# A hand-laid instruction order rewritten, with the last output projections of the first tile in two parts

## The chip, the core and the metric

The kernel runs on one core of a Trainium2 chip. The metric is the device time of one execution in microseconds (us). The work is spread over TensorE (PE: matrix products, with PEld for the loading of weights), VectorE (DVE), ScalarE (ACT) and GpSimd (POOL); SyncE (SP) issues nearly all DMA transfers. Each engine takes its instructions in program order and waits at an instruction until what it needs is there.

## What is computed

An attention over keys and values that are averaged over groups of eight, and behind it two gated layers. The weights but one arrive as float64, all else as float32; the products are fp32 products, or sums of three products of high and low parts.

```python
k_p = k.reshape(B, H, Sp, 8, D).mean(axis=3); v_p = ...   # B, H, S, D = 4, 8, 576, 64
attn = softmax(q @ k_p.T / sqrt(D)); x = attn @ v_p        # x becomes 2304 x 512
xn = x / sqrt(mean(x * x) + 1e-6) * rms_g
g, val = xn @ w_gate, xn @ w_val                           # 512 -> 1536
x = (silu(g) * val) @ w_out                                # 1536 -> 512
out = ((x @ w_a) * (x @ w_b)) @ w_out2                     # 512 -> 1536 -> 512
```

## The kernel before

Tokens are taken in blocks of 128 (S0 to S17). The first layer works on them in four stretches: a first tile of 512 tokens, a second of 256, and two slices of 768 (`TILES1`). The second layer then takes three slices of 768.

The two stages up to the second layer are written out by hand. `FIRST` (line 129) and `SECOND` (line 31) are lists of tokens; `token` (line 778) runs one token after another, and the instructions that a token makes join the queues of their engines in that order. So a list sets, for each engine and for the DMA queue of SyncE, the order of its work, and nothing else reorders it (`manual_schedule`, from line 1598). Waits come from the data alone. The parts of a token's name:

- `K`, `L`, `y`, `z` load the keys and values of batch 0 to 3, `q` a block of queries, `l` one weight part (lines 265 to 380 and 596). `k`, `w` sum keys and values of batch 0 by eights on VectorE (`w0!` on GpSimd), `b` and `t` spread them into blocks; `p`, `r`, `u` are the same steps of the later batches. `N` makes the negated identity (line 749). `W` is the warming: products of the identity with itself into two banks (line 754).
- `S` followed by block and step is attention of a block: `.0` scores (PE), `.1` maximum (DVE; from block 4 on also the difference), `.8` subtraction of the maximum as a product (PE, blocks 0 to 3), `.2` exponential (ACT), `.3` transposes (PE), `.4` their copy (ACT), `.5` values (PE), `.6` division (DVE), `.7` squares (ACT), `R` the root (DVE), `.9` scaling (DVE), `.10` transposes (PE), `.11` high part (ACT), `.12` low part (DVE). A trailing `a` or `b` is half of such a step, `@acc0` and the like name the PSUM bank it borrows.
- `c0` to `c3` convert one weight part from float64 (line 609): two ScalarE instructions, two on VectorE (`c1`, `c2`, lines 637 and 649), and an addition (`c3`, line 656) on GpSimd, or on VectorE where the token ends in `!`. There are 36, three for each of the 12 pieces of the hidden layer: gate, value, output. `D` writes a converted output weight back to memory.
- `s`f`.0h`, `s`f`.0l` split a gate weight into a high part (ScalarE, line 692) and a low part (line 696: GpSimd, or VectorE with `!`); `s`f`.1` is the value weight.
- `g`, `v` are the gate and value products of a job of the first tile, in two halves `a` and `b` of three products for each of two pieces (line 706); `a` is the gate's activation, `h` its product with the value on VectorE, `o` the output projection: fp32 products of four pieces (line 711). There are 14 jobs: pieces 0 and 1 in halves of 256 tokens (jobs 0 to 3), pieces 2 to 11 whole (jobs 4 to 13).

In `SECOND`, `G`, `V`, `A`, `H`, `W`, `Y`, `O` are the same work for the second tile (line 1325; here the output projection takes parts, and a low part of an output weight is `W`f`l`), `E` copies out the first tile's result, `M` and `N` are the products of the two slices, `Q` and `U` their output projections (`Qe`, `Ue` copy a bank out, line 1564), `Z` prepares the second layer, and `||` opens the stage of the slices with banks of its own (line 1610). A bank of PSUM is placed in the order in which its name is first used in a stage.

An `!` moves a step to the other of GpSimd and VectorE (or a copy from ScalarE to VectorE, line 259).

## Time and profile before

| | us |
|---|---|
| median of three runs | 955.52 |
| the three runs | 953.97, 955.52, 955.97 |
| the profiled execution | 956.15 |
| its span, first to last instruction | 954.4 |
| TensorE busy in that span | 932.6 |
| mean granted clock of TensorE | 0.997 of 2.4 GHz |

The profiled execution's time lies 1.75 us above its span (the start and the end around it), and 0.63 us above the median. A row of a timeline gives the start from the span's beginning, the duration, the engine and the line of the kernel, what is written from what, and in brackets how long the engine was idle before it and what ended that. Neighbouring instructions of one form are merged (x8), and a fp32 product makes two records. Matrix products overlap, so a row's end is later than the next row's start.

### The profile page before, as it was taken

To read this page: it belongs to the slowest core of one execution; us is meant where nothing else is said; L and a number is where in the kernel's file an instruction comes from. 1 tells how busy PE (TensorE), PEld (TensorE's weight loads), DVE (VectorE), ACT (ScalarE), POOL (GpSimd) and SP (SyncE) were. 2 spreads that over 40 slices of the span, in tenths; PEclk is the share of its full clock that TensorE was granted. 3 is DMA by queue.
4 is the path that set the end of the run, shared out by engine and by line. 5 is a ranking of instruction groups with operands and counts; after the bars stand their busy time and mean duration, and the time that the engine had idled before them with its cause. 6 is when DMAs were issued, how large, how long until landed. Compare 5 with 4: busy or idle time off the path is not lost. (4 is left out here: it accounts for less than half of the span.)

```text
span 954.4 us, 14742 instructions
## 1 busy us (share of the span) xinstructions
PE 932.6 (98%) x5242; PEld 852.4 (89%) x5242; DVE 630.4 (66%) x1094; ACT 486.4 (51%) x943; POOL 342.2 (36%) x319
## 2 busy tenths in 40 slices
...
GB/s 293 198 248 265 176 81 130 172 127 42 48 58 72 42 174 122 143 76 154 149 223 106 154 104 150 131 140 127 142 154 136 127 116 229 183 165 100 157 108 66
DMA packets 67944, 133.34 MB, mean 140 GB/s; under 512 B 7456, under 2 KB 31264, under 8 KB 67872
## 3 DMA queue, kind: packets, MB, share of 16 engines
...
q8 instruction: 41, 0.67, 0.3%
q10 hardware_dynamic: 288, 0.39, 0.1%
...
## 5 line engine op out<-in xcount | busy, mean ns | idle before, releaser
L1203 DVE TENSOR_TENSOR hl<-hf,hh 128x768 fp32r<-128x768 f32 x36 | 35.5, 991 | 90.9 <-ACT hh L1202 90.9
L1225 PE MATMUL o<-wol,hh 128*128 128x512 f32 x216 | 84.0, 389 | 0.0
L1225 PE MATMUL o<-woh,hh 128*128 128x512 f32 x216 | 84.0, 389 | 0.0
L1225 PE MATMUL o<-woh,hl 128*128 128x512 f32 x216 | 84.0, 389 | 0.0
L1202 ACT CAST hh<-hf 128x768 fp32r<-128x768 f32 x36 | 30.0, 838 | 82.0 <-PE o L1225 74.6
L656 POOL TENSOR_TENSOR w<-w,st 128x512 int32<-128x512 int32 x20 | 26.2, 1309 | 113.1 <-DVE w L649 111.9
L1559 PE MATMUL o<-hh,wol 128*128 128x512 f32 (+1 forms) x192 | 65.1, 339 | 0.4 <-DVE wol L1533 0.4
L1559 PE MATMUL o<-hl,woh 128*128 128x512 f32 (+1 forms) x192 | 64.6, 337 | 0.5 <-DVE hl L1546 0.5
L1559 PE MATMUL o<-hh,woh 128*128 128x512 f32 (+1 forms) x192 | 64.8, 337 | 0.0
L1130 ACT COPY p<-X 128x384 f32<-128x384 f32 x36 | 17.3, 481 | 88.7 <-PE X L1122 88.7
L696 POOL TENSOR_TENSOR wl<-wf,wh 128x512 fp32r<-128x512 f32 x25 | 35.5, 1425 | 49.7 <-ACT wh L692 40.4
L656 POOL TENSOR_TENSOR wo<-wo,st 128x512 int32<-128x512 int32 x18 | 24.3, 1349 | 67.3 <-DVE wo L649 38.9
L626 ACT ACTIVATE st<-st 128x512 int32<-128x512 uint32 x72 | 48.2, 670 | 0.0
L1225 PEld LDWEIGHTS o<-woh,hh 128*128 128x128 f32 x216 | 40.6, 188 | 8.4
L1225 PEld LDWEIGHTS o<-wol,hh 128*128 128x128 f32 x216 | 40.6, 188 | 8.3
L1225 PEld LDWEIGHTS o<-woh,hl 128*128 128x128 f32 x216 | 40.6, 188 | 8.3
L714 PE MATMUL acc<-ht,wo 128*128 128x512 f32 (+1 forms) x112 | 43.0, 531 | 0.0
L1122 PE MATMUL X<-xh_t,bl 128*128 128x384 f32 x120 | 40.8, 340 | 1.2 <-DVE bl L1487 0.7
L1122 PE MATMUL Y<-xh_b,rl 128*128 128x384 f32 x120 | 41.1, 342 | 0.9 <-ACT p L1427 0.7
L1122 PE MATMUL X<-xh_b,al 128*128 128x384 f32 x120 | 40.5, 337 | 1.5 <-DVE ev L261 1.5
L1122 PE MATMUL X<-xh_t,rl 128*128 128x384 f32 x120 | 40.6, 338 | 1.0 <-ACT u L1130 1.0
L1158 DVE TENSOR_TENSOR u<-u,Y 128x384 f32<-128x384 f32 x36 | 19.8, 550 | 32.3 <-ACT u L1130 15.4
...
## 6 DMA issues: line engine op xcount, KB each, us to landing
...
```

What stands on the lines that cost most here:

```text
L626: nc.scalar.activation(out=low, in_=low.bitcast(U32), func=AF.Copy, scale=2.0 ** -29)
L656: (nc.vector if boot["alt"] else nc.gpsimd).tensor_tensor(out=bits, in0=bits, in1=low, op=ALU.add)
L696: (nc.vector if boot["alt"] else nc.gpsimd).tensor_sub(wl, wf[ph, f, i], wh.bitcast(F32))
L714: nc.tensor.matmul(accs[c][:, cols], w[:, c, :], ht[:, :cols.stop - cols.start], start=(f == 0 and cols.start == 0), stop=(f == NF - 1),)
L1122: nc.tensor.matmul(dst[:, :HALF], w[:, c0 + c, :], x[:, c, :], start=(start and i == 0), stop=(stop and i == 5), skip_group_check=True,)
L1130: nc.scalar.copy(t, src[:, :HALF])
L1158: nc.vector.tensor_add(u2, u2, Y[:, :HALF])
L1202: nc.scalar.copy(hh, hf)
L1203: nc.vector.tensor_sub(hl, hf, hh.bitcast(F32))
L1225: nc.tensor.matmul(accs[i], x[:, sub], y, start=(f == 0 and j == 0), stop=(f == NF - 1 and j == 2),)
L1559: nc.tensor.matmul(dst, w[:, c, :], x, start=(f == 0 and j == 0 and at == 0), stop=(f == NF - 1 and j == 2), skip_group_check=True,)
```

## The change

Both lists are laid out anew. `FIRST` has the same tokens and twelve more; `SECOND` has the same tokens. In both some tokens gain or lose their `!`: in `FIRST` 17 instead of 12 low parts of gate and value weights are on VectorE, in `SECOND` 8 instead of 4 low parts of output weights, and `t2`, the last of the mask products, goes to GpSimd. The last three output projections of the first tile (jobs 11 to 13) take high and low parts of weight and hidden value: `s9.2`, `s10.2`, `s11.2` split the weights, `x` and `y` the hidden values, into spare buffers of the tiles of x. `WARM` goes from 20 to 17; the loop makes `WARM // 2` products for each of two banks. The cut lists below show `FIRST` whole, and of `SECOND` the beginning, the change of stage and the end.

```diff
-WARM = 20
+WARM = 17
...
 SECOND = """
-y0 y1 r0 y2 B0 r1 S6.0 G0a s13.0h s13.1h W0c r2 S6.1 y3 G0b s13.1l! B1 E1 E0 S6.2 s13.0l S7.0 E0>
-V0a E2 s14.0h V0b S7.1 r3 y4 S6.3 E1> E2> S7.2 S6.4 y5 r4 S7.3 S7.4 S6.5 A0 E3 G1a S6.6 G1b y6 E3>
-S7.5 H0 s14.1h Y0c W0l B2 s15.0h Y0l S7.6 V1a r7 s14.0l W1c V1b s14.1l A1 H1 S8.0 B3 W1l! Y1c G2a
-s15.0l G2b q9 r8 S8.1 r5 V2a S6.7 A2 s16.0h O0a s15.1h S7.7 s15.1l! S9.0 Y1l! q10 S9.1 V2b G3a z0
...
-M0.e4 Ft1l! Fd1 || M0.3 M0.1 M1.1 Fd2 S13.3 M0.cr M0.p1 M1.e1 M1.3 M0.d1 M0.lr! S13.4 S12.3 M0.2
-T2> M1.e2! S12.4 Ft2c Fb11c Ft2l M1.e3 M1.cs M1.e4 M1.p1 S13.5 S13.6 q15 M0.4 Ft3c Fb11l M0.p5
...
-U11.x U11.h0 U11.k0 U10.4 U11.1 Zb11l U11.0 U11.k1! Ue0! Zt3l Zt2l U11.4 Zt4c Z0.la Ue0> Zt4l U11.2
-Ue1 Ue1> Ue2! U11.3 Ue3 Ue4 U11.5 Ue5 Ue5> Ue4> Ue2> Ue3> Z0.lb
+S6.0 s13.1h y0 E0! S6.1 s13.0h S7.0 r0 S6.2 G0a G0b B0 y1 B1 S7.1 E1! E0> E2 y2 r1 B2 s13.0l s13.1l
+S6.3 W0c S7.2 E2> S6.4 V0a S7.3 s14.0h E1> S7.4 s14.0l y3 A0 W0l E3 V0b r2 r3 H0 S6.5 G1a s14.1h
+W1c B3 s14.1l S6.6 G1b Y0c s15.0h V1a V1b q9 S7.5 Y0l! E3> y4 S7.6 A1 H1 G2a G2b y5 s15.0l! S8.0
+W1l q10 s15.1h S6.7 Y1c V2a s15.1l! B4 B5 S8.1 O0a r7 O0b r8 s16.0h S9.0 A2 Y1l! W2c S8.2 s16.0l!
+q11 S7.7 O1a O1b V2b S9.1 W2l H2 S8.3 r4 S9.2 G3a R6! G3b S8.4 S9.3 W3c r5 V3a V3b y6 s16.1h Y2c
...
+T0 T1 M0.e3 S13.3 M0.ls! Fd1 T3 S13.4 || M0.cr M1.e1 M0.1 M1.1 M1.e2 M0.2 M0.lr! q14 T1> Ft2c Fb11l
+M1.cs M1.ls! M0.3 M1.3 M1.e3 Ft2l M1.p1 M2.e1 T0> M1.e4 M0.p1 Ft3c M2.e2 M0.p5 S12.3 T3> T2> M1.2
...
+U10.k1! U9.5 U11.f2 U10.x! U10.h0 U9.2 U11.h1 U10.5 U11.h0 U10.k0 U11.w Z0.lr! U10.2 U11.k1! U10.1
+U10.3 Z1.ls! U10.0 U11.k0! U11.x! U11.1 U10.4 Zt2l! U11.0 Ue0 U11.2 U11.5 U11.3 U11.4 Ue1 Ue2 Ue0>
+Ue3! Ue4! Ue5! Zt4c Ue3> Z0.ls Ue5> Z1.lb Zt4l Ue4> Ue1> Ue2>
 """.split()
 FIRST = """
-K0 K1 W N k0 K2 K3 k1 k2 k3 b1a K4 b1b b0a q1 S0.0a@att S0.1a b0b S0.0b S1.0a@acc0 S1.1a S1.0b
-S1.1b S0.8a K5 w0! S0.1b w1 S1.8a q2 S0.2a S1.8b t0! S1.2a S0.8b S1.2b l K6 S2.0@acc1 L0 S0.2b t1!
-l w2 c0 S0.3a@acc0 c1 c2 t2 p0 l L1 S1.3a@att S1.3b S0.3b q3 S0.4a S0.4b c0 S0.5a@acc0 S1.4a S2.1
-S0.5b S2.8 c0 S1.4b l c3 c1 S2.2a S1.5a@att S2.2b c2 c1 S1.5b S2.3a@acc1 l S0.6 p1 G c2 S1.6 S0.7
-S2.3b S3.0@acc0 c3 S3.1 S2.4a c0 S1.7 c1 s0.1h R0 c2 S3.8 s0.0h l S0.9 S2.4b S3.2a S2.5a@att
-S3.3a@acc1 c0 S3.2b S0.10@v c3 c1 S0.11 c3 S1.9 q4 L2 S2.5b L3 S3.4a s0.0l s0.1l c2 S3.3b p2
-S1.10@g S3.5a@acc0 S3.4b S3.5b S1.11 l S0.12 p3 S1.12 c0 S2.6 g0a s1.0h p7 S2.7 g0b v0a p8 S3.6
-S3.7 s1.0l! v0b a0 R2 c3 q5 S4.0@acc1 c0 h0 S2.9 g1a g1b s1.1h S2.10@att S3.9 s1.1l! S3.10@acc0
-S2.11 a1 c1 S3.11 v1a v1b S2.12 c2 S5.0@att q6 S3.12 g2a h1 c1 c2 l L4 c0 D0 g2b a2 S4.1 l c1 c0 c1
-c2 c3 L5 v2a v2b h2 l c3 s2.0h c3! g3a c2 c3! l c0 o0 c1 l g3b a3 c2 D1 v3a s2.1h l s2.0l c3! v3b
-g4a D2 o1 c0 g4b s3.0h h3 s2.1l! v4a c0 c0 c1 q7 a4 c2 p4 v4b c1 l c3 c2 c1 c0 s3.0l g5a s3.1h l
-g5b c3! o2 c2 l c1 D3 c3! s3.1l! c2 c0 h4 s4.0h c3! c1 c0 o3 c2 c1 c2 v5a a5 l c3! s4.0l p5 v5b c0
-s4.1h l L6 S4.2 l c0 c3 l h5 c1 g6a c2 o4 S5.1 s4.1l! g6b v6a c3 c1 c2 l v6b c3! c0 c0 l c1 c2
-s5.0h s5.0l! a6 c3! g7a c0 q8 c1 g7b c2 s5.1h s6.0h c3! o5 D4 h6 s5.1l! c1 l c0 c1 s6.0l! l c2 v7a
-c3 s6.1h c2 c0 c0 c3! S4.3@att l c1 v7b c1 a7 s7.0h D5 c2 s6.1l! c3 c2 g8a S5.2 D6 c0 c3 h7 g8b
-s7.0l! a8 p6 l s7.1h c0 l c0 s7.1l c1 v8a c2 c3! v8b h8 l c1 g9a c2 c0 S4.4 p9 o6 l c1 g9b c3!
-S4.5@att s8.1h v9a c0 s8.0h l a9 c1 c2 c2 c0 c3 s8.0l! l c1 v9b S4.6 c2 g10a c1 s8.1l S5.3@att h9
-c3 s9.0h g10b S5.4 c0 D7 c3 S5.5@att c2 l D8 a10 v10a v10b c1 c2 s9.1h S4.7 S5.6 s9.0l l c3! o7
-S5.7 R4 c3! c0 l c1 S4.9 l c2 g11a c0 g11b c3! c0 s10.0h h10 s9.1l S5.9 c1 c1 S4.10@att s10.0l
-S4.11 c2 v11a v11b S4.12 c0 a11 s10.1h g12a c3! c2 s10.1l D10 c3 l o8 h11 c0 S5.10@att S5.11 c1 D9
-s11.0h g12b c2 c1 a12 v12a c3! v12b s11.1h c2 c3 s11.0l! s12.1h g13a o9 D11 g13b s11.1l s12.0h h12
-S5.12 o10 v13a a13 v13b o11 h13 o12 s12.1l o13 s12.0l
+K0 k0 K1 k1 W K2 q1 k2 K3 b0a b1a k3 b1b S0.0a@att S1.0a@acc0 K4 N l b0b S0.1a q2 S1.0b c0 S0.8a
+S1.1a S0.0b S1.1b S0.1b S1.8a K5 S0.2a l K6 S1.2a l S0.8b S1.8b c1 S0.2b w0! c2 S0.3a@acc1 S0.4a w1
+c3 c0 t0! L0 S2.0@att S1.2b S0.3b S2.1 S0.4b w2 c1 G c0 l p0 S1.3a@acc0 L1 S2.8 S0.5a@acc1 t1!
+S1.4a s0.0h c1 c2 t2! S1.3b S2.2a c2 S2.2b q3 c3 S0.5b S1.5a@att S1.4b l S2.3a@acc0 s0.1h S0.6
+S1.5b p1 S1.6 S2.3b S2.4a S3.0@acc1 S3.1 S2.4b L2 c3 S0.7 S1.7 p2 S3.8 R0 c0 L3 S2.5a@att q4 S3.2a
+S3.3a@acc0 s0.0l S2.5b c1 c0 S0.9 S0.10@v S1.9 c2 S3.2b S3.4a S0.11 l S3.3b c1 l S1.10@g S1.11
+S3.4b c3 c0 p3 S0.12 q5 s0.1l S3.5a@acc1 S3.5b S1.12 S2.6 s1.0h L4 p7 g0a p8 S2.7 S3.6 g0b q6 S3.7
+v0a c2 c3! s1.0l R2 a0 S4.0@acc0 v0b h0 g1a s1.1h S2.9 c0 g1b s1.1l! q7 l S2.10@att v1a S2.11 S3.9
+c1 S3.10@acc1 S3.11 S2.12 c2 a1 c0 S3.12 v1b S5.0@att g2a S4.1 c3 c1 L5 h1 g2b l o0 c2 a2 c0 v2a c1
+c3! l v2b c1 c2 g3a o1 c3! c0 c2 l h2 l s2.0h c3! D0 l c1 g3b s2.1h s2.0l! v3a c0 c2 s2.1l! c1 c3!
+a3 c2 c0 v3b q8 l s3.0h h3 g4a c3! l c1 g4b v4a v4b s3.1h c0 s3.0l! s3.1l a4 p4 c1 g5a c2 c0 S5.1
+c3 c1 c2 c2 g5b D1 c0 h4 S4.2 c3 S5.2 s4.0h o2 s4.0l! c1 v5a a5 c3 l l c0 l c2 v5b c0 c3! s4.1h l
+c1 c2 c1 c3 g6a c2 S4.3@att c3 c0 o3 s5.0h s4.1l! D2 l l S4.4 g6b c1 a6 h5 c2 c3! o4 c0 c0 v6a
+s5.1h s5.0l! c0 s5.1l v6b c1 l c0 g7a p5 c1 c2 h6 c1 g7b c2 D3 c2 c3 L6 p6 l v7a c3 l v7b o5 s6.0h
+a7 s6.1h c3! l c1 D4 s6.0l c2 p9 c0 c3! s7.0h c0 c1 g8a D6 S4.5@att g8b D5 s6.1l! c2 c3 c0 h7
+s7.0l! v8a a8 c1 c2 c3! l S4.6 v8b l c0 c1 c0 c2 l c3! S5.3@att g9a c1 s7.1h s7.1l c2 c3 h8 S5.4
+S5.5@att c1 c0 s8.0h o6 S5.6 s8.1h s8.0l! S5.7 l g9b c1 c2 l S4.7 c0 v9a c1 c3! l D8 c2 c3! c0 v9b
+c2 s8.1l! R4 c1 a9 s9.0h s9.0l! g10a S4.9 c2 g10b h9 c0 c3! s9.1h c1 S5.9 l l o7 v10a s9.1l!
+S4.10@att v10b c0 c2 c3 c1 a10 c0 g11a c2 l h10 c3! S4.11 c1 S4.12 c3! c2 s10.0h c3! g11b s9.2h l
+a11 s10.1h c0 v11a s10.2h s10.0l v11b c1 c0 c2 l h11 s10.1l! g12a c3 c1 c2 o8 x11 s11.0h D7 c0
+s10.2l S5.10@att g12b a12 v12a s12.0h c1 v12b y11 o9 s11.0l g13a h12 c3 S5.11 x12 s9.2l S5.12 D9
+o10 s11.1h s11.1l! c2 D10 g13b o11 s12.1h c3! s11.2h y12 v13a s12.0l! v13b a13 s12.1l! h13 x13 D11
+o12 y13 s11.2l o13
 """.split()
...
             ht = state[j, "ht"]
             nc.vector.tensor_mul(ht[:, :m], ht[:, :m], state[j, 1][:, :m])
 
+        def spare():
+            if "spare" not in state:
+                state["spare"] = [
+                    x_p.tile([P, KD, 512], F32R, tag=tag, name=f"parts_{tag}") for tag in ("xh", "xl")
+                ]
+            return state["spare"]
+
+        def out_part(j, low):
+            f = jobs[j][0]
+            base = 2 * (j % 2)
+            hi, lo = [
+                spare()[0][:, base + e].rearrange("p (c f) -> p c f", c=KD) for e in range(2)
+            ]
+            if not low:
+                nc.scalar.copy(hi, wf[0, f, 2])
+                state[j, "w"] = (hi, lo)
+            else:
+                (nc.vector if boot["alt"] else nc.gpsimd).tensor_sub(lo, wf[0, f, 2], hi.bitcast(F32))
+
+        def hidden_part(j, low):
+            hi, lo = [spare()[1][:, 2 * (j % 2) + e] for e in range(2)]
+            if not low:
+                nc.scalar.copy(hi, state[j, "ht"])
+                state[j, "x"] = (hi, lo)
+            else:
+                nc.vector.tensor_sub(lo, state[j, "ht"], hi.bitcast(F32))
+
         def project_out(j):
             if not accs:
                 accs.extend(new_accs())
             f, cols, last = jobs[j]
+            if (j, "x") in state:
+                (wh, wl), (hh, hl) = state[j, "w"], state[j, "x"]
+                for c in range(KD):
+                    for i, (w, x) in enumerate(((wl, hh), (wh, hh), (wh, hl))):
+                        nc.tensor.matmul(
+                            accs[c], w[:, c, :], x, start=False, stop=(f == NF - 1 and i == 2)
+                        )
+                return
             out_direct(wf[0, f, 2], f, accs, state[j, "ht"], cols)
 
         for j in range(len(jobs)):
             names[f"v{j}b"] = lambda j=j: half(j, 1, 2)
             names[f"h{j}"] = lambda j=j: hidden(j)
             names[f"o{j}"] = lambda j=j: project_out(j)
+            for e in range(2 if j > 7 else 0):
+                names[f"s{jobs[j][0]}.2{'hl'[e]}"] = lambda j=j, e=e: out_part(j, e)
+                names[f"{'xy'[e]}{j}"] = lambda j=j, e=e: hidden_part(j, e)
         for i in range(2):
             for f in range(2 * NF):
                 names[f"s{f}.{i}h"] = lambda f=f, i=i: split_w(0, f % NF, i, 0)
```

## Rows read from the trace of the kernel before

**Rows 1.** The page's first part: busy time, share of the span and instructions of each engine

```profile
PE 932.6 (98%) x5242; PEld 852.4 (89%) x5242; DVE 630.4 (66%) x1094; ACT 486.4 (51%) x943; POOL 342.2 (36%) x319
```

**Rows 2.** Windows by stage (us, busy (x instructions) by engine, clock, DMA share, GB/s)

```profile
3.00:18.00 15.00, 13.07 (x79) 11.61 (x78) 9.20 (x16) 3.86 (x10) 4.83 (x8) 1.00 1.04 387
20.00:100.00 80.00, 73.69 (x387) 58.70 (x387) 76.53 (x141) 60.98 (x110) 26.09 (x19) 1.00 0.68 230
100.00:145.00 45.00, 45.00 (x195) 32.03 (x194) 25.52 (x49) 20.06 (x38) 19.52 (x14) 1.00 0.39 123
...
169.00:536.00 367.00, 364.34 (x2310) 348.34 (x2309) 274.99 (x492) 227.00 (x466) 176.34 (x178) 1.00 0.35 111
```

**Rows 3.** TensorE's timeline, 0:38 (start, us, instruction, [idle before <-releaser])

```profile
1.93 7.39 PE L758 MATMUL warm_up<-ident 128*128 128x128 f32 x40 [1.93 <-POOL ident masks.py:199]
...
10.45 1.22 PE L422 MATMUL sc<-KB,q 128*128 128x144 f32 x8 [0.64 <-DVE m L443]
...
36.48 0.36 PE L706 MATMUL g<-xh,wl 128*128 128x256 f32 x1 [2.13 <-DVE rs L501]
```

**Rows 4.** VectorE's timeline, 0:38

```profile
7.45 0.75 DVE L336 TENSOR_REDUCE kp<-kv_xl 128x72 f32<-128x576 f32 x1 [0.71 <-DMA kv_xl<-in_k_dram]
...
9.85 0.46 DVE L443 TENSOR_REDUCE m<-sc 128x4 f32<-128x288 f32 x1 [1.23 <-PE sc L422]
...
13.01 0.94 DVE L443 TENSOR_REDUCE m<-sc 128x4 f32<-128x288 f32 x2 [0.85 <-PE sc L422]
...
28.29 0.74 DVE L520 SCALAR_TENSOR_TENSOR x<-x,br,gain 128x512 f32<-128x512 f32 x1
28.95 1.51 DVE L637 TENSOR_SCALAR wf<-wf 128x512 int32<-128x512 int32 x1
30.39 1.75 DVE L520 SCALAR_TENSOR_TENSOR x<-x,br,gain 128x512 f32<-128x512 f32 x1
32.06 1.76 DVE L649 SCALAR_TENSOR_TENSOR wf<-st,wf 128x512 int32<-128x512 int32 x1
...
35.67 0.67 DVE L541 TENSOR_TENSOR xl<-xP,xh 128x512 fp32r<-128x512 f32 x1
```

**Rows 5.** GpSimd's timeline, 0:38

```profile
30.14 3.14 POOL L696 TENSOR_TENSOR wl<-wf,wh 128x512 fp32r<-128x512 f32 x2
```

**Rows 6.** ScalarE's timeline, 70:80.5

```profile
77.23 0.60 ACT L692 CAST wh<-wf 128x512 fp32r<-128x512 f32 x1
77.85 1.28 ACT L809 ACT_TABLE_LOAD   x1
```

**Rows 7.** TensorE's waits, 37:157 (line <- releaser: us in total, times, longest)

```profile
PE g L706 <- ACT ht L809: 0.6, 1, 0.6
```

**Rows 8.** TensorE's timeline, two product rows at 58, the late projections

```profile
58.36 0.39 PE L706 MATMUL v<-xh,wl 128*128 128x512 f32 x1
58.59 0.39 PE L706 MATMUL v<-xh,wh 128*128 128x512 f32 x1
...
145.15 10.46 PE L714 MATMUL acc<-ht,wo 128*128 128x512 f32 x24
```

**Rows 9.** TensorE's timeline, the seam to the second tile

```profile
162.76 0.77 PE L468 MATMUL eP<-ident,E 128*128 128x128 f32 x5 [0.78 <-ACT eT L473]
164.30 3.08 PE L491 MATMUL av<-VB,eT 128*128 128x130 f32 x12 [0.78 <-ACT eT L473]
167.14 0.56 PE L706 MATMUL g<-xh,wl 128*128 128x256 f32 x1
```

**Rows 10.** The window 166:168 (columns as in rows 2)

```profile
166.00:168.00 2.00, 2.00 (x10) 2.00 (x10) 0.51 (x3) 0.94 (x2) 0.98 (x1) 0.51 0.36 132
```

**Rows 11.** TensorE's timeline, the seam to the second layer

```profile
537.88 0.41 PE L1122 MATMUL X<-xh_b,al 128*128 128x384 f32 x1 [1.48 <-DVE ev L261]
```

**Rows 12.** VectorE's timeline, the same seam

```profile
534.24 2.89 DVE L1041 TENSOR_TENSOR xl_t<-x,xh_t 128x384 fp32r<-128x384 f32 x6
537.05 0.68 DVE L261 COPY ev<-o 128x512 f32<-128x512 f32 x1
```

More of the change, by code (lines that the diff above doesn't have):

```diff
@@ new lines @@
+S9.4 B6 A3 s17.0h s16.1l! S8.5 Y2l! H3 G4a z0 W3l! S8.6 Y3c G4b s17.0l! S6.9 V4a r6 A4 V4b G5a
+S6.10 O2a H4 O2b S6.11! r9! Y3l s17.1h G5b z1 s18.0h Y4c W4c S6.12! O3a W4l! B7 s17.1l u0 S9.5 O3b
+s18.1h S8.7 s18.1l! V5a B8 q12 z2 S9.6 A5 Y4l! s19.0h W5c u1 O4a W5l! s18.0l V5b S7.9 S9.7 G6a
+S10.0 G6b s19.0l! H5 V6a V6b s20.0h A6 Y5c S10.1 s19.1h s20.1h S10.2 S11.0 q13 s19.1l O4b s20.0l!
+B9 S11.1 H6 G7a z3 G7b u2 S11.2 S10.3 Y5l! S10.4 O5a z4 s20.1l V7a S11.3 R8 A7 V7b W6c G8a S9.9
+S8.9 Y6c H7 S11.4 G8b S7.10 V8a s21.0h S7.11! Y6l S7.12! V8b u3 z5 A8 S10.5 s21.1h s21.0l! O5b
```

168 lines of the change are left out of this document (80 added, 88 removed).

## The prediction

> **What bounds the kernel now.** I read the page's engine line first: TensorE is busy for 932.6 of 954.4 us [rows 1], so a new order of the same work can win only what TensorE loses to waits, plus what its work shrinks by. The windows by stage say where that is: in 20:100 VectorE works 76.5 of 80 us while TensorE loses 6.3; in 169:536 TensorE loses only 2.7 of 367 [rows 2]. So three spots matter. At the start only attention runs until the first gate product at 36.48 [rows 3], and VectorE sets that moment. At the seam between the first tile and the second TensorE waits for two attention blocks, and at the seam to the second layer for a copy. Elsewhere the path is TensorE's own queue.
>
> **The start.** The warming ends at 1.93 + 7.39 = 9.32, the first maximum at 9.85 + 0.46 = 10.31; the score products at 10.45 wait 0.64 for it, and the last two maxima end at 13.01 + 0.94 = 13.95 [rows 3, 4]. From there to 36.34, where the low part of the second block ends (35.67 + 0.67), the VectorE timeline has no gap: 22.4 us of work. Three instructions in it, at 28.95, 30.39 and 32.06, took 1.51, 1.75 and 1.76 us; the one before them, of the same size and kind, took 0.74 [rows 4]. The last two begin as GpSimd's pair of 30.14 begins and goes on, and end 0.5 us after each of the pair does (31.7 and 33.28) [rows 5]. The loss is at least 5.02 - 3 x 0.74 = 2.8 us.
>
> What the new list does there: the first score halves of both blocks and the second of block 1 stand ahead of the first maximum, so fewer products stand between maxima. The second q load goes ahead of the fourth k load. At 387 GB/s [rows 2] 256 KB take 0.68 us, so the k sum of 7.45 starts at 8.1 and ends at 8.9; the negated identity, moved behind it, fills the 1.23 us that VectorE idles ahead of 9.85 [rows 4]. It costs nothing under that cover, and one small instruction, under 0.8, without it. The first maximum still ends at about 10.3. Behind it stand one subtraction product and one score half, about 0.6 each (half of the 1.22 at 10.45), and a maximum of 0.46 [rows 3, 4]: the last one ends at 12.0, 1.9 earlier than 13.95. On SyncE's queue a weight load and the third q load move ahead of the second v load and delay it by 768 KB, 2.0 us. Counted from 3.0, where the window of that rate begins, the 3.54 MB up to its end take 9.1 us, so it lands at 12.2 or a little later, and VectorE reaches its sums at 13.1, behind the first weight part's two steps. The delay costs nothing under that cover, and up to 2.0 without it.
>
> Behind that VectorE has one mask product less (it goes to GpSimd), 0.3 us, and one merge that only moves past this point. So its queue ends 1.9 + 0.3 = 2.2 us sooner if all three stretches stay, 5.0 if none does. GpSimd's two weight-low parts no longer follow one on the other there: the first comes as soon as its cast is there, the second behind the first block's low part. One stretch looks left, which makes about 4. TensorE can use that only if what follows is ready. The activation ahead of the gate product of the fifth weight pair (a5) now stands behind two softmax exponentials and a table load of 1.28 us [rows 6], and the low parts s2.0, s3.0 and s4.0, which were GpSimd's, each stand on VectorE just ahead of the gate product that needs them. I take **3.0 us** for the start, between 2.2 and 4 because these three low parts have no time to spare; bounds 0 and 5.6, the upper with the 0.6 that TensorE waits once for an activation [rows 7]. Two of ScalarE's table loads go. They hide behind TensorE and count for nothing alone; without that cover each was 1.28.
>
> The warming products: 17 // 2 is 8 for each of two banks, so 16 remain of 20, not 17. They took 7.39 us [rows 3]; a fifth less is at most 1.5 us, but the first maximum, which waits for the k sums and the moved identity, sets what follows, so I count nothing. Bounds: 0.6 gained, or the first two score halves at half speed, 0.6 each lost.
>
> **The last three output projections.** Now they are 24 records from 145.15 to 155.5, 10.3 us. In parts they are 36 products of the form whose records start 0.23 apart (58.36, 58.59) [rows 8]: 8.3 us, so **2.0 us** less on the path. The price is six casts of 0.60 on ScalarE [rows 6] and six subtractions, 0.67 on VectorE [rows 4] or about 1.6 on GpSimd (half of 3.14) [rows 5]. From 100 to 145 VectorE is busy for 25.5 of 45 us [rows 2], so they hide, except behind the last value product: the last hidden product, its cast and its low part follow one another, 0.67 + 0.60 + 0.67 = 1.9 us. The projection before covers 12 x 0.23 = 2.8 of that if its products start at once. If they must wait for the last job's cast, because both jobs' parts lie in one tile, 1.3 us is lost there and a low part of 0.67 behind it: the whole gain. Bounds 0 and 2.0.
>
> **The seam to the second tile.** Before, all four gate and value halves ran ahead of the first transposes. TensorE then waited 0.78 at 162.76 and at 164.30, ran the value products in 3.08 us [rows 9] with the clock at 0.51 in 166:168 (the 1.2 GHz level) after these idle stretches [rows 10], and reached the second gate at 167.14, 11.6 us after the projections. The new list issues both blocks' scores first, then two gate halves, and deals the two value halves between the transposes. Counted anew: two score blocks 2 x 1.1 (the eight records at 10.45) [rows 3], four halves of six records at half of 0.23, 2.8 in all [rows 8], two transposes at 0.7, value products 1.5 at full clock (half of 3.08) [rows 9]: 7.9, and about 1.1 of idle time while VectorE makes the second block's difference and the first gate's activation stands behind its table load. That is 9.0 instead of 11.6, **2.6 us**; bounds 0 and 3.7.
>
> **The seam to the second layer.** At 537.88 the first product waited 1.48 us [rows 11] for a copy that VectorE reached at 537.05, behind six subtractions begun at 534.24 [rows 12]. Banks go to a stage in the order in which it first names them: the first was Z0's, with that copy. In the new list it is X0's, copied on ScalarE early; the next product's bank waits for the third of three VectorE copies, about 0.4. So **1.1 us**; bounds 0 and 1.5.
>
> **The rest.** 169:536 is the same work in a new order; its waits were 2.7 us [rows 2]. All could go, or twice as many could come: I take no change, bounds -2.7 and +2.7.
>
> **Sum:** 3.0 + 2.0 + 2.6 + 1.1 = 8.7 us. The profiled execution took 956.15, 0.6 above the median of 955.52. 956.15 - 8.7 = 947.45; I forecast 947.5 and leave the 0.6 as slack, since a chain I did not walk can only be later.
>
> **Rivals.** *The start's gain is eaten* (0.19). VectorE is nearly full from 20 to 100 [rows 2], and the low parts moved to it have no time to spare; or the last projection waits for its parts. Then 3.0 to 5.0 of the 8.7 go: 950.5 to 952.5. For it speaks the 76.5 of 80 us; against it, that GpSimd has less to do and so stretches fewer.
>
> *Nothing moves* (0.08). The new order's waits take the place of the old ones, within 1.9 us of before: 953.6 to 957.4.
>
> *Slower, by blocked subtractions* (0.07). Seventeen weight-low parts of the first tile stand on VectorE instead of twelve, and eight of the second tile's output weights instead of four. Each that starts while GpSimd runs may wait for its end and lose about 1.3 us, as at 32.06 [rows 4, 5]. GpSimd is busy for 176 of 367 us in 169:536 [rows 2], so about half would meet it. It decides only where VectorE is late, and makes the kernel slower than before from seven on VectorE's path: 7 x 1.3 = 9.1 against 8.7; with nine it is 959. The Trainium skill has a rule for it ("SBUF — State Buffer", Who interferes with whom): VectorE and GpSimd share one port pair as an exclusive lock, and a VectorE instruction with two SBUF inputs waits for the end of a GpSimd instruction that reads SBUF. By that rule all these low parts would meet it; the trace agrees in the three stretched instructions, and no row read here shows a plain subtraction in that place.
>
> **Chances.** Forecast 0.66, its own range 942.5 to 950.5; eaten 0.19; same 0.08; slower 0.07. Faster by over 0.2% (1.9 us, about what a measurement of this kernel can tell from no change) is 0.66 + 0.19 = 0.85. The range 942.5 to 954 leaves out the slower cases and the far end of the bounds.
>
> **What would show it.** Right: the first gate product at 31 to 33; the three late projections as 36 records in 8.3 us; the granted clock at 1.00 through the seam to the second tile; no wait over 0.5 us at the seam to the second layer. Wrong: as many VectorE instructions of 1.3 us or more ahead of 60 as before; gate products that wait for a low part; a wait ahead of the last projection; more than 5 us of waits in the middle, or a second fall of the clock.

## The result and the profile after

The changed kernel takes **944.89 us** in the median of four runs (944.14 to 945.74), the kernel before 954.99 (953.97 to 955.97, four runs); the ratio is 0.9889, with a 95% interval of 0.9876 to 0.9901. The forecast was 947.5, so the direction and the range held and the gain was larger: 10.1 us instead of some 8. By steps it was right in some places and wrong in others: the start brought 2.4 us more than forecast and the middle 3.4 more, the two seams 1.5 and 2.2 less. That the sum came within 2.6 us of the forecast is therefore partly luck.

The profiled execution took 944.95 us, with a span of 943.2. The spans of the two profiled executions differ by 11.2 us, the medians by 10.1; the account below is of the spans. First the page's busy times:

```profile
PE 926.3 (98%) x5246; PEld 853.5 (90%) x5246; DVE 630.9 (67%) x1119; ACT 485.6 (51%) x944; POOL 313.9 (33%) x303
```

TensorE works 6.3 us less than in [rows 1]: 2.2 us in the stretch of the late projections, 1.7 in the warming, and 1.4 at the seam to the second tile, where no product runs at half clock any more; the second layer takes 0.6 more, since half clock comes there, and the rest is small differences elsewhere. What is left of the 11.2 us between the spans is waits. Windows by stage (columns as in rows 2):

```profile
20.00:100.00 80.00, 77.38 (x426) 62.48 (x425) 73.75 (x144) 60.02 (x110) 27.47 (x20) 1.00 0.71 230
...
148.00:160.00 12.00, 9.85 (x75) 8.97 (x74) 7.32 (x13) 7.49 (x13) 2.99 (x3) 1.00 0.58 188
160.00:524.00 364.00, 363.61 (x2311) 348.90 (x2310) 272.13 (x510) 227.35 (x466) 152.72 (x164) 1.00 0.36 114
...
536.00:542.00 6.00, 4.55 (x17) 4.55 (x18) 6.00 (x13) 3.91 (x10) 0.00 (x0) 0.72 0.07 26
```

In 160:524 TensorE loses 0.4 of 364 us, where it lost 2.7 of 367 [rows 2]. Two places lose time now: the seam to the second tile (148:160) and the one to the second layer, where TensorE first waits and then runs at a clock of 0.72 in the mean of 536:542. TensorE's timeline at the places of the prediction:

```profile
1.93 5.67 PE L759 MATMUL warm_up<-ident 128*128 128x128 f32 x32 [1.93 <-POOL ident masks.py:199]
...
31.08 0.36 PE L707 MATMUL g<-xh,wl 128*128 128x256 f32 x1
...
63.84 0.50 PE L707 MATMUL g<-xh,wl 128*128 128x512 f32 x1 [0.76 <-ACT ht L810]
...
142.51 5.61 PE L853 MATMUL acc<-parts_xl,parts_xh 128*128 128x512 f32 x24
147.96 1.14 PE L423 MATMUL sc<-KB,q 128*128 128x144 f32 x8
150.79 1.22 PE L423 MATMUL sc<-KB,q 128*128 128x144 f32 x8 [1.69 <-issue]
...
156.81 1.77 PE L492 MATMUL av<-VB,eT 128*128 128x130 f32 x12
158.59 0.36 PE L707 MATMUL g<-xh,wl 128*128 128x256 f32 x1
...
537.45 0.44 PE L1161 MATMUL Y<-xh_b,rl 128*128 128x384 f32 x1 [2.60 <-ACT p L1169]
```

The same marks in both timelines, in us, give the account of the difference:

| mark | before | after | change up to here | of this step |
|---|---|---|---|---|
| first gate product | 36.48 | 31.08 | -5.4 | -5.4 |
| first score product behind the late projections | 155.45 | 147.96 | -7.5 | -2.1 |
| second gate product of the second tile | 167.14 | 158.59 | -8.6 | -1.1 |
| end of the first layer's last product | 536.40 | 524.43 | -12.0 | -3.4 |
| first product of the output block | 802.37 | 791.48 | -10.9 | +1.1 |
| span | 954.4 | 943.2 | -11.2 | -0.3 |

### The profile page after: what moved, and what is told of

The parts are those of the page before. It is cut to its first block, busy times and chain, and to the rows that moved or that the text cites. A ratio compares the mean times of both kernels' runs of the same rounds, so it can differ in the third digit from the quotient of the medians.

```text
span 943.2 us, 14755 instructions
## 1 busy us (share of the span) xinstructions
PE 926.3 (98%) x5246; PEld 853.5 (90%) x5246; DVE 630.9 (67%) x1119; ACT 485.6 (51%) x944; POOL 313.9 (33%) x303
## 4 chain that ended last, share of the span: by engine, by line
PE 87%; DMA 5%; DVE 4%; ACT 2%; issue 1%; SPq 1%; POOL 0%; DVEq 0%; ACTq 0%
PE X L1161 25%; PE o L1264 16%; PE Y L1161 13%; PE o L1598 9%; PE Z L1161 6%; PE v L707 4%; PE g L707 4%; PE acc L715 3%; PE av L492 3%; DMA st<-in_moe_w_out_dram 1%; PE acc L1415 1%; PE sc L423 1%; DMA st<-in_moe_w_val_dram 1%; PE eP L469 1%; DMA hf<-h 1%
## 5 line engine op out<-in xcount | busy, mean ns | idle before, releaser
L1598 PE MATMUL o<-hh,wol 128*128 128x256 f32 (+1 forms) x192 | 65.3, 340 | 0.1
L1598 PE MATMUL o<-hh,woh 128*128 128x256 f32 (+1 forms) x192 | 64.7, 337 | 0.0
L1598 PE MATMUL o<-hl,woh 128*128 128x256 f32 (+1 forms) x192 | 64.6, 336 | 0.0
L697 POOL TENSOR_TENSOR wl<-wf,wh 128x512 fp32r<-128x512 f32 x22 | 29.6, 1352 | 54.0 <-ACT wh L693 45.8
L1161 PE MATMUL X<-xh_t,sl 128*128 128x384 f32 x120 | 40.8, 340 | 0.0
L1161 PE MATMUL X<-xh_t,bh 128*128 128x384 f32 x120 | 40.6, 338 | 0.0
L1161 PE MATMUL X<-xl_t,bh 128*128 128x384 f32 x120 | 40.6, 338 | 0.0
```

The costliest lines, as they stand in the source:

```text
L697: (nc.vector if boot["alt"] else nc.gpsimd).tensor_sub(wl, wf[ph, f, i], wh.bitcast(F32))
L1161: nc.tensor.matmul(dst[:, :HALF], w[:, c0 + c, :], x[:, c, :], start=(start and i == 0), stop=(stop and i == 5), skip_group_check=True,)
L1598: nc.tensor.matmul(dst, w[:, c, :], x, start=(f == 0 and j == 0 and at == 0), stop=(f == NF - 1 and j == 2), skip_group_check=True,)
```

## Experiments

Every kernel was timed in alternation with the kernel before; "the changed kernel" stands for 944.89 us, ratio 0.9889. Differences of 1 us lie inside the intervals of the ratios, so the verdicts rest on the marks in the timelines. Line numbers differ by one where a list has one line fewer. Ten kernels share the start of the changed one up to its first gate product; that product comes at 30.04 to 31.08 in them, median 30.2, so the changed kernel's profiled execution has the latest start of them.

**1. The first tile alone.** Both lists hold the same tokens, but for the parts of the late projections, so either can stand with the other.

```
-SECOND = """ (new order)
+SECOND = """ (order of before)
```

> The changed kernel with the second list of before, so only the first tile (start, late projections) is new. Theory A (the gains add up place by place: start 5.4, projections 2.1, seam and middle 3 to 4, second layer a loss of 1 to 2): the first gate product stays at 31.1 and the last projection ends at 148; the second gate product comes 11.5 to 11.7 later as before, with a clock of about 0.5 behind the waits; time 946.5 to 948 us. Rival B (a queue carries lateness from the first tile into the second, so the old second list fits the new first one badly): over 949 us.

Measured: 948.89 us (947.29 to 952.22), ratio 0.9937 (0.9920 to 0.9954). The first gate product stands at 30.28, the late projections end at 147.09; from there to the second gate product it takes 12.7 us, more than the 11.7 of before, because a new wait appears:

```profile
159.75 0.36 PE L706 MATMUL g<-xh,wl 128*128 128x256 f32 x1 [2.04 <-ACT ht L1376]
```

From the first layer's end (530.29) to the output block (796.34) it takes 266.1 us, as before (266.0). So the first tile is worth some 6 to 7 us and the second list 4. The time lies between the two ranges: the gains add up, less about 1 us that the old second list loses behind the new first one.

**2. The late projections in fp32 again.** Six casts and six subtractions go, the products are L714's again.

```
-... s9.2h ... s10.2h ... x11 ... s10.2l ... y11 ... x12 s9.2l ... s11.2h y12 ... x13 ... y13 s11.2l o13
+(without these twelve tokens)
```

> The changed kernel with its last three output projections whole in fp32 again, without the six casts and six subtractions. Theory A (they are on TensorE's path and nothing hides them): 3.43 instead of 2.7 us each, 2.1 us slower than the changed kernel, 947.0 us, and the wait for the score bank at the seam moves along. Rival B (the seam behind them waits for something that does not depend on them): under 0.7 us slower.

Measured: 947.42 us, ratio 0.9916 (0.9902 to 0.9930), 2.5 more. From the first gate product to the scores behind the projections it takes 149.44 - 30.39 = 119.05 us, against 116.88 in the changed kernel: 2.2 us. The wait of 1.69 at the seam comes along unchanged. Theory A.

**3. Another bank for the second scores.**

```
-S6.0 s13.1h y0 E0! S6.1 s13.0h S7.0 r0 ... S7.1 E1! E0> E2
+S6.0 s13.1h y0 E0! E1 S6.1 s13.0h S7.0@acc0 r0 ... S7.1 E0> E2
```

> The changed kernel with the seventh block's scores of the second tile in the accumulator pair acc0, which is emptied by then, instead of the att pair, and the second eviction moved ahead of them to ScalarE. Theory A (the wait of 1.69 us at 150.79 and the one at 153.74 are for the pair of banks that both blocks' scores share, held until VectorE's subtraction): the scores follow the first ones at 149.1 without a wait, the transposes start 1.7 to 2.1 us earlier, second gate product at 156.5 to 157.0 instead of 158.6, time 942.8 to 943.3. Rival B (the wait is for the q load, the k sums or the exponent): the scores still start at 150.8, time as the changed kernel, 944.9.

Measured: 943.32 us, ratio 0.9878 (0.9862 to 0.9894). TensorE's timeline at the seam:

```profile
148.26 2.12 PE L422 MATMUL sc<-KB,q 128*128 128x144 f32 x16
...
154.46 0.76 PE L468 MATMUL eP<-ident,E 128*128 128x128 f32 x5 [1.22 <-ACT eT L473]
...
158.18 0.36 PE L706 MATMUL g<-xh,wl 128*128 128x256 f32 x1 [0.40 <-ACT ht L1376]
```

Both blocks' sixteen score products now run without a gap: the 1.69 us labelled "issue" were the bank, which VectorE held until its subtraction for the first block was done. In the changed kernel that subtraction ends at 149.93 + 0.76 = 150.69, and the second scores start at 150.79:

```profile
149.93 0.76 DVE L446 TENSOR_TENSOR E<-sc,m 128x576 f32<-128x576 f32 x1
```

So a wait can come from a bank that two blocks share, and not from the data alone. But only 0.7 of them reach the second gate product (9.92 us behind the first scores instead of 10.63); the rest comes back as waits for the other block's copy and for the gate's activation. The cause is shown, the size of theory A was too large.

**4. The chain of that seam cleared.** Two attempts came first:

```
-S6.0 s13.1h y0 E0! S6.1 s13.0h S7.0 r0 S6.2 G0a G0b B0 y1 B1 S7.1 E1! E0> E2 y2 r1
+S6.0 s13.1h E0! E0> E1 y0 S6.1 s13.0h S7.0@acc0 r0 S6.2 E2 E2> G0a G0b B0 y1 B1 S7.1 y2 r1
...
-S6.3 W0c S7.2 E2> S6.4 V0a S7.3
+S6.3 S6.4 S7.2 W0c V0a S7.3
```

> The kernel of the bank experiment, and besides: the first two sends of the evicted tile directly behind their copies, the third copy ahead of the second block's scores' copy, and the first block's transposed copy ahead of the second block's exponential on ScalarE. Theory A (after the scores' bank the next two limits are the transposes' bank, which waits for ScalarE's copy, and the gate's buffer, which waits for a send): from the first scores to the second gate product 8.7 to 9.2 us, against 10.63 in the changed kernel and 9.92 with the bank alone; 942.4 to 943.0 us. Rival B (the chain of scores, maximum, exponential, transposes and values of two blocks has no slack left): 9.7 to 10.0 us, 943.3.

Measured: 947.32 us, ratio 0.9914 (0.9900 to 0.9927), 12.1 us from scores to gate: the weight's load B0, now behind the sends, came late, its cast waited 1.48 us for it ahead of the second copy, and the clock fell to 0.50. Neither theory had that.

```
-S6.0 s13.1h E0! E0> E1 y0 S6.1 s13.0h S7.0@acc0 r0 S6.2 E2 E2> G0a G0b B0 y1 B1 S7.1 y2 r1
+S6.0 s13.1h E0! E0> E1 B0 S6.1 s13.0h S7.0@acc0 y0 r0 S6.2 E2 E2> G0a G0b y1 B1 S7.1 y2 r1
...
-S6.3 S6.4 S7.2 W0c V0a S7.3 s14.0h E1> S7.4 s14.0l
+S6.3 S6.4 S7.2 V0a S7.3 S7.4 W0c s14.0h E1> s14.0l
```

> The seam experiment again without its mistake: the output weight's load keeps its early place in SyncE's queue and its cast stands behind both blocks' transposed copies on ScalarE. Theory A: no ScalarE wait for a weight between the two exponentials and the second transposed copy; from the first scores to the second gate product 8.9 to 9.4 us, clock 1.00, 942.4 to 943.2 us. Rival B (the gate's activation behind its table load sets the second gate product whatever stands ahead): 9.7 to 10.0 us, as with the bank alone, 943.3.

Measured: 946.77 us (944.51 to 947.78), ratio 0.9910 (0.9894 to 0.9926), 11.0 us in the profiled execution, which at 944.51 is the fastest of its five: no wait for a weight any more, but the key sum between the two blocks' maxima and two casts ahead of the gate's activation were still there. The third attempt moved those:

```
-S6.0 s13.1h y0 E0! S6.1 s13.0h S7.0 r0 S6.2 G0a G0b B0 y1 B1 S7.1 E1! E0> E2 y2 r1
+S6.0 s13.1h y0 B0 y1 B1 E0! E0> E1 S6.1 s13.0h S7.0@acc0 S6.2 E2 E2> G0a G0b S7.1 r0 y2 r1
...
-S6.3 W0c S7.2 E2> S6.4 V0a S7.3 s14.0h E1> S7.4 s14.0l y3 A0 W0l E3 V0b r2 r3 H0 ... S6.6 G1b
+S6.3 S6.4 S7.2 V0a S7.3 E1> S7.4 y3 A0 s14.0h W0c s14.0l W0l E3 V0b H0 ... S6.6 r2 r3 G1b
```

> The changed kernel with the bank experiment's edit, and the work that stood between the links of the chain at the seam moved behind it: the key sum between the two blocks' maxima, the two casts ahead of the second transposed copy and of the gate's activation, the two key sums ahead of the first hidden product; the first block's transposed copy ahead of the second exponential; the sends of the evicted tile directly behind their copies, the loads at their old place. Theory A (the links themselves, two blocks' maxima, differences, exponentials and copies, take about 8 us and the rest was work of others that stood in their queues): 8.0 to 8.8 us from the first scores to the second gate product, against 10.63 in the changed kernel and 9.92 with the bank alone; 942.2 to 943.2 us. Rival B (what is moved comes due at once behind the chain: waits for key sums and casts between 160 and 175 take the gain back): second gate product early, but the first layer's end no earlier than with the bank alone; 943.3 or more.

Measured: 943.13 us (942.86 to 943.56), ratio 0.9879 (0.9863 to 0.9896).

```profile
146.87 2.12 PE L422 MATMUL sc<-KB,q 128*128 128x144 f32 x16
...
152.50 0.77 PE L468 MATMUL eP<-ident,E 128*128 128x128 f32 x5 [0.65 <-ACT E L461]
...
155.83 0.36 PE L706 MATMUL g<-xh,wl 128*128 128x256 f32 x1
...
535.90 0.44 PE L1160 MATMUL Y<-xh_b,rl 128*128 128x384 f32 x1 [3.00 <-ACT p L1168]
```

The seam takes 8.96 us, 1.7 less than in the changed kernel, a little over what theory A gave. But from the first scores to the first layer's end it is 375.6 us here, 375.4 in experiment 3 and 376.5 in the changed kernel: half of the 1.7 is taken back on the way, as rival B had it, though not where it said (one wait of 0.60 us, up to 517.31, is far behind the seam). Then the wait at the seam to the second layer is 3.00 us, and 2.05 in experiment 3. The two kernels are alike, and the fastest measured: 1.6 and 1.8 us under the changed kernel by the medians, with no run of either above the lowest of that one (944.14); the intervals of the ratios overlap with its own. That the last kernel's lead comes from its seam is mostly not shown: its first scores stand at 146.87 instead of 147.96, and up to there both kernels run the same first list. From the first scores to the end of the span it takes 794.9 us here, 795.2 in the changed kernel and 793.2 in experiment 3.

**5. Whether the sends hold up the second layer.** ScalarE's and VectorE's timelines of the changed kernel show what the 2.60 us wait for:

```profile
535.51 0.51 ACT L911 CAST xh_t<-x 128x384 fp32r<-128x384 f32 x1 [0.73 <-DVE x L920]
536.51 0.51 ACT L911 CAST xh_t<-x 128x384 fp32r<-128x384 f32 x1 [0.48 <-DVE x L920]
536.93 0.47 ACT L1169 COPY p<-Y 128x384 f32<-128x384 f32 x1
```

```profile
534.87 0.56 DVE L920 TENSOR_TENSOR x<-x,x 128x384 f32<-128x384 f32 x1 [1.62 <-DMA x<-x]
535.92 0.56 DVE L920 TENSOR_TENSOR x<-x,x 128x384 f32<-128x384 f32 x1 [0.49 <-DMA x<-x]
```

The copy of Y's bank stands behind casts of the second column tile's x, these behind differences, and these wait for the loads of x. On SyncE those stand behind eight sends of the swept tile.

```
-Ue1 Ue2 Ue0> Ue3! Ue4! Ue5! Zt4c Ue3> Z0.ls Ue5> Z1.lb Zt4l Ue4> Ue1> Ue2>
+Ue1 Ue2 Ue0> Ue1> Ue2> Ue3! Ue4! Ue5! Zt4c Ue3> Z0.ls Ue4> Z1.lb Zt4l Ue5>
```

> The changed kernel with the two sends Ue1 and Ue2 moved from the end of SyncE's queue to their evictions, and Ue4 ahead of Ue5. Theory A (the 2.60 us at 537.45 is ScalarE's copy behind casts that wait for x loads, and these stand on SyncE behind the sends): the loads start at about 527 instead of 528.97, the wait falls to 0.7 or less, the clock stays at 1.00 in 536:546; 2 to 3.5 us faster than the changed kernel, 941.4 to 942.9. Rival B (the loads wait for their buffers or for DMA bandwidth, not for the queue): the same wait within 0.5 us, 944.4 to 945.

Measured: 944.07 us, ratio 0.9881 (0.9867 to 0.9895). SyncE's queue and the wait:

```profile
521.32 2.52 SPq L1610 DMA_DIRECT2D x<-ev  x4
524.24 3.39 SPq L1613 DMA_DIRECT2D x<-ev  x4
527.68 3.79 SPq L898 DMA_DIRECT2D x<-x  x8
```

```profile
536.72 0.69 PE L1160 MATMUL Y<-xh_b,rl 128*128 128x384 f32 x1 [2.81 <-ACT p L1168]
```

Counted from the second layer's first product the loads start 0.3 us earlier, and the wait is as long. The time is rival B's, but its reason (buffers or bandwidth) is not shown. In either order all eight sends stand ahead of the loads: from the first send to the first load it takes 6.7 us in the changed kernel (522.27 to 528.97) and 6.4 here, of which 2.7 and 1.1 are waits for copies of the swept tile. So this edit took little of the cause away; experiment 7 shows that the loads can start earlier.

**6. The casts behind the copies.**

```
-        group(1, 0, steps[2:])
+        group(1, 0, idle * 6 + steps[2:9] + [lambda: [f() for f in steps[9:]]])
```

> The changed kernel with the side work of the second group of the second layer moved three slots later, so that the casts of the second column tile's x stand behind the group's three snapshots on ScalarE instead of between them. Theory A (the 2.60 us is the snapshot's place behind casts that wait for x): no wait over 0.5 us there, clock 1.00 in 536:546, 941.0 to 942.4 us. Rival B (the x parts are needed themselves by then, and the wait moves to the next group's products on them): waits of 2 us or more between 535 and 545 in another place, 944.0 to 945.0.

Measured: 947.87 us, ratio 0.9920 (0.9907 to 0.9934). The wait is gone from its place and comes back twice as long:

```profile
546.45 0.69 PE L1161 MATMUL X<-xh_t,sl 128*128 128x384 f32 x1 [5.56 <-ACT p L1169]
```

By the place of the wait this is rival B, but the time lies above its range: the clock falls as well, to 0.61 in 544:548, and from the second layer's first product to the output block it takes 270.6 us instead of 267.2. The next group needs these parts, and making them is some 10 us of work on VectorE from the moment that x is there.

**7. The loads ahead of the sends.** SyncE's order was written out for the first two groups, for which their part of the program became a scheduling block of its own.

```
-Ue1 Ue2 Ue0> Ue3! ... Ue1> Ue2>
+Ue1 Ue2 Ue0> Ue3! ... (without the other sends)
...
+        sends = [lambda i=i: names[f"Ue{i}>"]() for i in range(1, 6)]
-        group(0, 0, loads + idle * 3 + steps[:2])
+        group(0, 0, [lambda: [f() for f in loads], lambda: [f() for f in sends]] + idle * 3 + steps[:2])
         group(1, 0, steps[2:])
+        yield
```

> The changed kernel with SyncE's queue ordered by hand at the seam to the second layer: the eight loads of the second column tile's x stand directly behind the first send, and the other sends of the swept tile behind them. Theory A (the wait there is for x, which is late because loads and sends share one queue and the DMA engines, and the casts and differences on VectorE follow its arrival): loads land 3 us or more earlier, no wait of 1 us or more between 530 and 550, clock 1.00 there; from the first layer's end to the output block 263.5 to 264.8 us instead of 267.0; 941.5 to 943.0 us. Rival B (the loads cannot start earlier, because their buffers are still read by the last forms of the first layer's end): they issue at 527 or later and the sends behind them are late as well; 944.5 to 946.

Measured: 945.66 us, ratio 0.9901 (0.9885 to 0.9918).

```profile
522.28 3.78 SPq L898 DMA_DIRECT2D x<-x  x8
...
531.62 0.40 SPq L1220 DMA_DIRECT2D h<-u  x1
```

```profile
534.27 0.93 ACT L910 CAST xh_b<-x 128x384 fp32r<-128x384 f32 x2 [5.51 <-DMA h<-u]
```

The loads start 4.7 us before the 527 of rival B, and the last of them, issued by 526.1, lands within 5.3 us, so all are there by 531.4. Yet the first cast waits until 534.27, by the profile for a store of hidden rows, and the order on TensorE changed as well (the next group's first product stands within this one). TensorE now waits twice, 1.39 us up to 534.84 and 1.29 up to 546.3, with the clock at 1.00, and from the first layer's end to the output block it takes 267.5 us (267.0 in the changed kernel). That is neither theory: this run tells that the loads can start earlier; whether that gives the time back it doesn't decide.

**8. GpSimd beside VectorE at the start.** First in the kernel before, by parting the pair of [rows 5]:

```
-S2.5a@att S3.3a@acc1 c0 S3.2b ... S3.4a s0.0l s0.1l c2
+S2.5a@att S3.3a@acc1 s0.0l c0 S3.2b ... S3.4a s0.1l c2
```

> The kernel before with one token moved: the low part of the first gate weight goes to GpSimd's queue some 20 tokens earlier, so that the pair of 3.14 us at 30.14 no longer stands together. Theory A (GpSimd's work stretches the VectorE instructions of 1.51, 1.75 and 1.76 us and these cost the first gate product 2.8 us): at most one stretched instruction is left, first gate product at 33.7 to 35.0 instead of 36.5, 952.0 to 953.7 us. Rival B (the changed kernel's earlier start comes from its order of products and maxima; stretched instructions wait for each other anyway): first gate product at 36.0 or later, 954.5 to 955.5.

Measured: 955.51 us, ratio 1.0 (0.9991 to 1.0009), first gate product at 37.12. VectorE's and GpSimd's timelines:

```profile
26.29 1.24 DVE L564 TENSOR_TENSOR by<-by,ba 128x2 f32<-128x2 f32 x1
27.56 1.21 DVE L569 SCALAR_TENSOR_TENSOR br<-by,br 128x2 f32<-128x2 f32 x1
...
30.54 1.51 DVE L637 TENSOR_SCALAR wf<-wf 128x512 int32<-128x512 int32 x1
31.97 1.75 DVE L520 SCALAR_TENSOR_TENSOR x<-x,br,gain 128x512 f32<-128x512 f32 x1
```

```profile
26.23 1.27 POOL L696 TENSOR_TENSOR wl<-wf,wh 128x512 fp32r<-128x512 f32 x1 [4.59 <-ACT wh L692]
27.46 1.28 POOL L656 TENSOR_TENSOR wo<-wo,st 128x512 int32<-128x512 int32 x1
```

The numbers are rival B's, but not for its reason: the moved low part now runs beside two steps of the square root, of two columns each, which take 0.16 us elsewhere. They end at 27.53 and 28.77, each 0.03 behind an end on GpSimd (27.50 and 28.74). One stretch of 1.1 us went and two of 1.1 us came, and VectorE's work from the last maximum to the second low part takes 23.4 us instead of 22.4. The gate product is not VectorE's alone here: that low part ends at 36.84, and TensorE, which ran at a granted clock of 0.50 in 30:36 (the 1.2 GHz level) behind an idle stretch of 3.41 us, ends the products ahead of the gate just before 37.12.

Then the other way, in the changed kernel:

```
-S1.4a s0.0h c1 ... c3 S0.7 S1.7 p2 S3.8 R0
+S1.4a c1 ... c3 S0.7 S1.7 s0.0h p2 S3.8 R0
```

> The changed kernel with the cast of the first gate weight moved behind the second block's squares, so that its low part runs on GpSimd while VectorE works through the twelve short steps of the square root (24.4 to 26.5) instead of at 22.3. Theory A (a VectorE instruction with two SBUF inputs waits for the end of a GpSimd instruction in progress): one or two of the short steps take 1.0 to 1.3 us instead of 0.16, the root takes 3.1 us or more instead of 2.1, first gate product 0.8 to 1.3 us later, 945.5 to 946.2. Rival B (no such wait; the stretched steps of before came from something else): root 2.1 us, 944.9.

Measured: 946.28 us, ratio 0.9904 (0.9890 to 0.9919), first gate product at 31.40, 1.2 behind the median of the ten, though only 0.3 behind the changed kernel's own, whose first k sum came late (8.42; here 7.61, and 7.43 to 7.96 in the others).

```profile
23.71 0.16 DVE L555 TENSOR_SCALAR ba<-ss 128x2 f32<-128x2 f32 x1
23.91 1.13 DVE L558 TENSOR_SCALAR br<-ba 128x2 int32<-128x2 int32 x1
...
29.31 0.74 DVE L336 TENSOR_REDUCE kp<-kv 128x72 f32<-128x576 f32 x1
```

```profile
23.71 1.29 POOL L696 TENSOR_TENSOR wl<-wf,wh 128x512 fp32r<-128x512 f32 x1 [2.46 <-ACT wh L692]
...
29.19 1.35 POOL L656 TENSOR_TENSOR wf<-wf,st 128x512 int32<-128x512 int32 x1 [4.18 <-ACT xh L534]
```

One step takes 1.13 instead of 0.17 and ends 0.04 behind GpSimd's; the root takes 3.1 us, and VectorE's work from the last maximum to the second low part 19.7 us instead of 19.1. Theory A in effect, though the stretched step has one tensor input, not two. A reduction inside GpSimd's 29.19 to 30.54 takes its usual 0.74.

**9. The warming.**

```
-WARM = 17
+WARM = 20
```

> The changed kernel with 20 warming products instead of 16. Theory A (the first maximum waits for the k sums and the moved identity, so warming hides): first gate product within 0.5 us of 31.1, 944.4 to 945.4 us. Rival B (the warming stands on the path to the first scores): 1.4 us later, 946.0 to 946.6.

Measured: 944.19 us, ratio 0.9880 (0.9866 to 0.9893), first gate product at 30.47, among the ten. Theory A: the length of the warming costs nothing here.

## Why the prediction was right, and where not

*The start: 3.0 forecast, 5.4 measured.* The mechanism was right and the size too small. The last maximum ends at 11.40 + 0.46 = 11.86, as forecast (12.0), 2.1 us earlier than before. The step "One stretch looks left" failed: none is left. VectorE's and GpSimd's timelines of the changed kernel:

```profile
11.40 0.46 DVE L444 TENSOR_REDUCE m<-sc 128x4 f32<-128x288 f32 x1 [0.20 <-PE sc L423]
...
26.73 1.41 DVE L521 SCALAR_TENSOR_TENSOR x<-x,br,gain 128x512 f32<-128x512 f32 x2
28.06 0.69 DVE L650 SCALAR_TENSOR_TENSOR wf<-st,wf 128x512 int32<-128x512 int32 x1
28.66 0.42 DVE L638 TENSOR_SCALAR wf<-wf 128x512 int32<-128x512 int32 x1
28.99 0.75 DVE L337 TENSOR_REDUCE kp<-kv 128x72 f32<-128x576 f32 x1
29.66 1.28 DVE L542 TENSOR_TENSOR xl<-xP,xh 128x512 fp32r<-128x512 f32 x2
```

```profile
22.27 1.26 POOL L697 TENSOR_TENSOR wl<-wf,wh 128x512 fp32r<-128x512 f32 x1
28.88 1.35 POOL L657 TENSOR_TENSOR wf<-wf,st 128x512 int32<-128x512 int32 x1 [5.34 <-ACT xh L535]
```

The two scalings that took 0.74 and 1.75 [rows 4] take 1.41 together, the two conversion steps 0.69 and 0.42, and the reduction beside GpSimd's 28.88 its usual 0.75. The three stretched instructions had thus lost 3.2 us (1.75 - 0.70, 1.51 - 0.42 and 1.76 - 0.69), where the prediction had "at least" 2.8, and the queue from the last maximum to the second low part is 19.1 us instead of 22.4. Up to 60, five VectorE instructions took 1.2 us or more before, and none does now. Together the two causes give 2.1 + 3.2 = 5.3 of the 5.4 us; by the median of the ten kernels (30.2) the start would have gained 6.3. The end of the prediction's own bracket for no stretch, 5.0, was nearly it; I took 3.0 because three low parts had no time to spare. They cost nothing: the single wait up to the late projections is 0.76 for an activation, 0.6 before [rows 7]. Experiment 8 shows that a stretch that is added lengthens VectorE's work, by 1.0 and 0.6 us. That taking them away gave the 3.2 is read from the timelines; no run takes one away alone, or parts them from the 2.1 us of the maxima. Ten steps of blocks 0 to 4 also borrow another PSUM bank than before, and no run tells what that is worth.

*The late projections: 2.0 forecast, 2.1 measured* (experiment 2: 2.2 in the timeline). The last one follows without a wait; the feared order through one tile did not arise.

*The seam to the second tile: 2.6 forecast, 1.1 measured.* The clock stays at 1.00 and the value products take 1.77, both as forecast. What failed is "about 1.1 of idle time while VectorE makes the second block's difference": the second scores do not run beside the first block's maximum, they wait for its subtraction, since both blocks' scores use one bank pair. From the first scores to the first transposes it takes 5.8 us in both kernels (155.45 to 161.24, 147.96 to 153.74); and two of the four halves that covered it were moved out of it. Measured are 2.0 us of waits (1.69 and 0.31) instead of 1.1, and 8.6 of work instead of 7.9. A walk of the banks, which the prediction made only for the second layer, would have shown it.

The old order's waits at this seam, 2.1 us in all, are no longer than the new order's, so the 1.1 gained are the clock's alone. And the clock was not the order's alone either. The first kernel of experiment 8 has the old second list and the old waits, yet its clock stayed at 1.00 and its second gate product came 10.65 us behind the first scores, against 10.63 in the changed kernel (columns of the window as in rows 2):

```profile
164.13 1.77 PE L491 MATMUL av<-VB,eT 128*128 128x130 f32 x12 [0.78 <-ACT eT L473]
165.92 0.36 PE L706 MATMUL g<-xh,wl 128*128 128x256 f32 x1
```

```profile
166.00:168.00 2.00, 2.00 (x17) 2.00 (x18) 1.46 (x5) 1.34 (x4) 1.15 (x1) 1.00 0.39 133
```

In the old order the clock fell to about 0.5 in two of three profiled executions, in the new one in none of seven. That the new order keeps the clock up is likely by that, but not shown, and the forecast of a clock at 1.00 may have come true by luck.

*The seam to the second layer: 1.1 gained by forecast, 1.1 lost.* The wait of 1.48 [rows 11] is gone as said: the first product follows the sweep at once. The failed step is that nothing was asked about what comes next. The loads of x start 4.7 us behind the second layer's first product, where before three of eight started 2.6 ahead of it, and the differences on VectorE start 10.6 behind it instead of 8.5. TensorE meets them in the second group, waits 2.60, and 538:542 runs at a clock of 0.57. Removing the first wait only moved TensorE up to the next one; moving the casts (experiment 6) or two sends (experiment 5) did not remove it. Which of the loads, the differences and the casts sets this wait stays open.

*The rest: 0 forecast, 3.4 gained,* outside the bound of 2.7. Waits go from 2.6 to 0.2 us, and about 0.4 us was the half clock behind the old seam, which lasted past the mark at 167.14. The remaining half us I can't place; the marks do not cut the two orders at exactly the same work. Experiment 1 shows that it belongs to the second list.

Of the rivals, *the start's gain is eaten* did not come, nor did *slower by blocked subtractions*: such subtractions exist, but TensorE doesn't wait for them. The price of 1.3 us that this rival took for a stretch was too high: the instruction at 32.06 took 1.76 and takes 0.69 now, so it had lost 1.1. The Trainium skill's rule on this ("SBUF — State Buffer", Who interferes with whom) goes further than the part I had used: it also lists tensor_scalar, by its two-port modes, among the operations that can contend with GpSimd, and says that reductions never do on this chip. The 1.13 and 0.74 us of experiment 8 agree with both. Of the three stretched instructions of [rows 4], two have two SBUF inputs, as the prediction says of all; the one at 28.95 is a tensor_scalar with one. Of the signs of being wrong, a second fall of the clock came, at the seam to the second layer.
